# Two feed-forward layers behind a chunk attention: the second layer in a fixed order for each engine, products bank by bank at a block's ends, evictions on one engine

## The chip, the cores and the metric

The kernel runs on one core of a Trainium2 chip. The metric is the device time of one launch in microseconds (us). TensorE (PE) multiplies matrices, VectorE (DVE), ScalarE (ACT) and GpSimd (POOL) work on elements, SyncE (SP) issues the DMA transfers. Each engine works through its own list of instructions in order; semaphores tie the lists together.

## The reference, cut to what matters

```python
# q, k, v: [8 batches, 8 heads, 576, 64]; chunks of 64 positions
scores = scale * np.matmul(q_c, k_c.transpose(0, 1, 2, 4, 3))
attn = np.exp(scores - np.max(scores, axis=-1, keepdims=True))
attn = attn / (np.sum(attn, axis=-1, keepdims=True) + 1e-09)
x = (attn @ v_c), reshaped to [4608 tokens, 512]
h = x @ w_in                                  # layer 1: 512 -> 2048
g = np.maximum(h, 0.0) + alpha * np.minimum(h, 0.0)
x = g @ w_out                                 # 2048 -> 512
h = x @ w_in2                                 # layer 2: 512 -> 2048
g = h - np.tanh(h)
out = g @ w_out2                              # 2048 -> 512
```

All of it is float32. A product of two float32 matrices is made of three products of a high and a low half (high by high, low by high, high by low).

## The kernel before, in words

The 4608 tokens go through in 9 blocks of 512 (NB). The blocks j = 0 to 8 are layer 1, j = 9 to 17 layer 2; layer 1 leaves its results in DRAM (`ysc`) and layer 2 loads them again (`load_y`, L504) and splits them into halves `xh`, `xl` (L508 on ACT, L509 on DVE). The attention of later blocks, the loading and splitting of layer 1's weights and the conversion of layer 2's weights (stored to DRAM as `wm` at L170, fetched and split again from j = 8 on, L153 and L154) are pieces of work that a table of events (`at`, `fire`) places at the steps of the blocks.

A block has 16 steps (KF). Step f makes, for 128 of the 2048 hidden units,

- `up(f)`: 12 matmuls (L420) of 128x512 into one of two PSUM buffers, `hps`;
- `act_g(f)`: the activation, from `hps` to `g` in SBUF. In layer 1 that is two DVE instructions (L441, L444). In layer 2 it is `tanhshrink`: ACT makes `sq` (L460), `th` (L461) and `w` (L462); DVE makes a mask from `sq` (L464; its buffer is `ktc`), then L465, L466, L467, L468 and at last a predicated copy (L469) that picks, element by element, one of two results;
- `split_g`: `g` into two halves, `ghi` on ACT (L450) and `glo` (L451). `glo` is made on DVE in blocks 1 to 8, on POOL in layer 2. In layer 2 the Python code calls `split_g` one step late (`late`);
- `down(f-2)`: 12 matmuls (L478) of the step two before (LAG = 2) into four PSUM banks, `y0` to `y3`, that add up over the block. The first matmuls of a product take `ghi`, its last third `glo`.

The four banks are there once. At a block's end `finish` copies them to SBUF as `yst`, banks 0 and 2 on ACT (L495), banks 1 and 3 on DVE (L497), and SP stores them (L498). Because of the lag, `down(14)` and `down(15)` of a block run in steps 0 and 1 of the next one, and `down(0)` of the next one, in its step 2, is the first that needs the banks empty.

What sets the order: outside a few stretches marked `tc.manual_schedule()` a scheduler arranges the instructions of each engine when the kernel is built. So the order on an engine isn't the order in which Python calls. Inside `tc.manual_schedule()` the order is the program's. Before, only the start of the kernel and its last piece (the last `split_g` and the two last `down`) were marked so. `stage` is a pool of 7 buffers that `sq`, `g` and `yst` share.

Of the kernel before, what the change touches and what calls it, by code (L numbers as in the profile page):

```python
# [27 lines left out]
def kernel(  # L28
# [19 lines left out]
    nc = tc.nc  # L48
# [35 lines left out]
    def slot(f, which, shape, dtype):  # L84
        return wpool.tile(shape, dtype, tag=f"w{which}_{f}", name=f"w{which}_{f}")
# [281 lines left out]
    def att_t_early(t):  # L367

        p = ps.pop(t).rearrange("p h d -> p (h d)")
        tr = ps_h.tile([P, HP, P], F32, tag="h", name="ptr")  # L370
        for hp in range(HP):
            nc.tensor.transpose(tr[:, hp, :], p[:, hp * P:(hp + 1) * P], ident)
        pts[t] = stage.tile([P, HP, P], F32, tag="st", name="pte")
        return nc.scalar.activation(out=pts[t], in_=tr, func=AF.Copy)
# [37 lines left out]
    def up(f, x, n, cols=None, hp=None):  # L412
        if hp is None:
            hp = ps_h.tile([P, n], F32, tag="h", name="hps")
        w = wsplit[f, 0]
        cols = cols or slice(0, n)
        for i, (a, b) in enumerate(((0, 0), (1, 0), (0, 1))):
            for kk in range(KD):
                m = slice(kk * P, (kk + 1) * P)
                nc.tensor.matmul(  # L420
                    out=hp[:, cols], lhsT=w[:, a, m], rhs=x[b][:, kk, cols],
                    start=(kk == 0 and i == 0), stop=(kk == KD - 1 and i == 2),
                )
        return hp

    def act_g(layer, f, hp, n, spare_vector):
        if (layer == 1 or spare_vector) and f % 2:
            g = stage.tile([P, n], F32, tag="st", name="g")
        else:
            g = gpool.tile([P, n], F32, tag="g", name="g", bufs=1)  # L430
        if layer == 1:
            tanhshrink(g, hp, n, f)
        elif spare_vector:
            neg = stage.tile([P, 512], F32, tag="st", name="neg")[:, :n]
            nc.scalar.activation(out=neg, in_=hp, func=AF.Relu, scale=-1.0)
            nc.scalar.activation(out=g, in_=hp, func=AF.Relu)
            nc.vector.scalar_tensor_tensor(
                out=g, in0=neg, scalar=nalpha_sb[:, f:f + 1], in1=g, op0=ALU.mult, op1=ALU.add
            )
        else:  # L440
            nc.vector.tensor_scalar(  # L441
                out=g, in0=hp, scalar1=0.0, scalar2=alpha_sb[:, f:f + 1], op0=ALU.min, op1=ALU.mult
            )
            nc.vector.scalar_tensor_tensor(out=g, in0=hp, scalar=0.0, in1=g, op0=ALU.max, op1=ALU.add)  # L444
        hi = gpool.tile([P, n], F32R, tag="ghi", name="ghi")
        lo = gpool.tile([P, n], F32R, tag="glo", name="glo")
        return g, hi, lo

    def split_g(g, hi, lo, lo_engine):
        nc.scalar.activation(out=hi, in_=g, func=AF.Copy)  # L450
        lo_engine.tensor_tensor(out=lo, in0=g, in1=hi.bitcast(F32), op=ALU.subtract)  # L451

    def tanhshrink(g, hp, n, f):


        ca, cb, ce, cc = TS
        sq = att.tile([P, 2, n], F32, tag="qt", name="sq")[:, 0] if f % 2 else stage.tile([P, n], F32, tag="st", name="sq")
        w = att.tile([P, n], F32, tag=("p", "pt")[f % 2], name="w")
        th = vpool.tile([P, n], F32, tag="v", name="th")
        nc.scalar.activation(out=sq, in_=hp, func=AF.Square)  # L460
        nc.scalar.activation(out=th, in_=hp, func=AF.Tanh)  # L461
        nc.scalar.activation(out=w, in_=sq, func=AF.Square, bias=bias_sb)  # L462
        mask = ktc.bitcast(U32).rearrange("p u h c d -> p (u h c d)")[:, f % 2 * n:(f % 2 + 1) * n]
        nc.vector.tensor_scalar(out=mask, in0=sq, scalar1=0.375 ** 2, scalar2=None, op0=ALU.is_ge)  # L464
        nc.vector.scalar_tensor_tensor(out=g, in0=sq, scalar=cc, in1=hp, op0=ALU.mult, op1=ALU.mult)  # L465
        nc.vector.tensor_tensor(out=th, in0=hp, in1=th, op=ALU.subtract)  # L466
        nc.vector.scalar_tensor_tensor(out=g, in0=w, scalar=ce, in1=g, op0=ALU.add, op1=ALU.mult)  # L467
        nc.vector.scalar_tensor_tensor(out=g, in0=sq, scalar=ca, in1=g, op0=ALU.add, op1=ALU.mult)  # L468
        nc.vector.copy_predicated(g, mask, th)  # L469

    def down(layer, f, g, acc, cuts=((0, 4),)):
        w = wsplit[f, 1]
        for c0, c1 in cuts:
            for i, (u, x) in enumerate(((0, 0), (1, 0), (0, 1))):
                for t in range(c0, c1):
                    m = slice(t * P, (t + 1) * P)
                    lhsT, rhs = (w[:, u, m], g[x + 1]) if layer == 0 else (g[x + 1][:, m], w[:, u])
                    nc.tensor.matmul(  # L478
                        out=acc[t], lhsT=lhsT, rhs=rhs, start=(f == 0 and i == 0), stop=(f == KF - 1 and i == 2)
                    )  # L480
# [5 lines left out]

    ysc = {}

    def finish(layer, j, t0, acc):
        if layer == 0:  # L490
            ysc[j] = dram.tile([KD, P, NB], F32, name=f"ysc{j}")
        for i, a in enumerate(acc):
            st = stage.tile([P, 512], F32, tag="st", name="yst")
            if i % 2 == 0:
                nc.scalar.activation(out=st, in_=a, func=AF.Copy)  # L495
            else:
                nc.vector.tensor_copy(st, a)  # L497
            nc.sync.dma_start(out=ysc[j][i] if layer == 0 else out[t0 + i * P:t0 + (i + 1) * P, :], in_=st)  # L498
# [16 lines left out]
    LAG = 2  # L515
# [32 lines left out]
    for unit in units:  # L548
# [5 lines left out]
        elif t >= 9:  # L554
            last = base[t] - 3
# [26 lines left out]
    for i in range(2 * KF):  # L582
        f, which = divmod(i, 2)
# [17 lines left out]
    def fire(step):  # L601
        for todo in events.pop(step, ()):
            for fn, args in todo:
                fn(*args)

    with tc.manual_schedule():
# [43 lines left out]
        x0 = get_x(0)  # L650
# [46 lines left out]
        last_a = att_t_early(3)  # L697
# [7 lines left out]
        hp0 = up(0, x0, NB, slice(0, 2 * P))  # L705
# [5 lines left out]
        load_natural_early(8, (15, 0))  # L711

    queue, late = [], []

    def next_down():
        layer, f, g, acc, j, t0 = queue.pop(0)
        if f == 0:
            acc.extend(new_acc(layer, NB))
        last = layer == 1 and f == KF - 1
        down(layer, f, g, acc, ((0, 2), (2, 3), (3, 4)) if last else ((0, 4),))  # L720
        if f == KF - 1:
            finish(layer, j, t0, acc)

    for j, (layer, t0) in enumerate(plan):
        x = get_x(j)
        acc = []
        for f in range(KF):
            hp = up(0, x0, NB, slice(2 * P, NB), hp0) if j == f == 0 else up(f, x, NB)
            if len(queue) == LAG:
                next_down()  # L730
            if j == 0:
                if 0 < f < KF - 1:
                    split_w(f + 1, 0, nc.gpsimd)
                if f > 0:
                    split_w(f - 1, 1, nc.gpsimd)
                with tc.issue_after(last_a.ins) if f == 1 else nullcontext():
                    fire(f)
            g = act_g(layer, f, hp, NB, j == 0)
            queue.append((layer, f, g, acc, j, t0))
            if layer == 1:  # L740
                if late:
                    split_g(*late.pop(), nc.gpsimd)
                late.append(g)
            else:
                if j == 1 and f == 0:
                    split_w(KF - 1, 1, nc.gpsimd)
                split_g(*g, nc.gpsimd if j == 0 else nc.vector)
            if j > 0:
                fire(j * KF + f)
    with tc.manual_schedule():  # L750
        split_g(*late.pop(), nc.vector)
        while queue:
            next_down()


# [26 lines left out]
```

## Time and profile before

| | |
|---|---|
| median of 3 runs | 1731.82 us (1729.38 to 1732.12) |
| the profiled execution | 1729.36 us |
| its span, first to last instruction | 1727.6 us |
| PE busy | 1670.8 us, 97%, 9389 matmuls |
| DVE, ACT, POOL busy | 77%, 40%, 20% |
| mean granted TensorE clock | 0.988 of full speed |

Stages by the clock of the span: to about 182 us the start with attention and weights, then layer 1; layer 2 accumulates its first block from 930 us; the last block starts to accumulate at 1637.6 us. A busy share of 97% on PE says that PE is nearly always at work, but a matmul's modelled end overlaps the next one's start, so a small idle time between two matmuls is read from the distance of their starts.

### The profile page before, as it was taken

The page shows a single profiled execution, that of the slowest core. Times are in us where ns is not written, and L with a number is a line of the kernel's source. Part 1 is how long each engine was busy: PE and PEld are TensorE (multiplying, and loading weights), DVE is VectorE, ACT ScalarE, POOL GpSimd, SP SyncE. Part 2 cuts the span into 40 slices and gives each one's busy share as a digit, 9 for nine tenths or more (in the row PEclk, how much of TensorE's full clock was granted, in tenths as well). Part 3 has the DMA queues.
Part 4 walks back from the last instruction along what each step waited for, and adds up shares of the span by engine and source line. Part 5 has one row for each costly group of instructions (what it writes and reads, how often), then busy time and mean ns, then how long its engine had stood idle before and what let it go on. Part 6 is the DMA issues. An engine that isn't in the chain of part 4 may idle for free.

```text
span 1727.6 us, 24773 instructions
## 1 busy us (share of the span) xinstructions
PE 1670.8 (97%) x9389; PEld 1360.8 (79%) x9389; DVE 1324.7 (77%) x2163; ACT 689.5 (40%) x1304; POOL 352.3 (20%) x264
## 2 busy tenths in 40 slices
PE   8877999999999999999999999999999999999998
PEld 7665788788887888888888778888888888888886
DVE  7988866778667868684437797978787878888776
ACT  6665422333322424231334444435353434344433
POOL 3663100000000000000243222222222222222221
PEclk9988999999999999999999999999999999999999
DMA  9811404433153514320422010101010101000000
GB/s 245 253 55 43 133 13 105 116 86 98 50 111 67 156 28 135 57 92 1 146 74 74 1 49 1 49 1 49 1 49 1 49 1 49 1 25 1 25 1 25
DMA packets 215591, 108.58 MB, mean 63 GB/s; under 512 B 170912, under 2 KB 187312, under 8 KB 215472
## 3 DMA queue, kind: packets, MB, share of 16 engines
q1 hardware_dynamic: 215472, 107.01, 22.8%
q8 instruction: 73, 1.20, 0.3%
q14 instruction: 46, 0.38, 0.1%
HBM read 79.70 MB, written 27.26 MB: 62 GB/s over the span
## 4 chain that ended last, share of the span: by engine, by line
PE 51%; DVE 21%; ACT 8%; issue 5%; SPq 3%; DMA 3%; POOL 0%; ACTq 0%; DVEq 0%; POOLq 0%
PE y L478 25%; PE hps L420 24%; DVE g L467 4%; DVE g L469 4%; DVE g L468 4%; DVE g L465 3%; SPq L232 3%; ACT ghi L450 2%; ACT sq L460 2%; DVE ktc L464 2%; ACT w L462 2%; DMA rw<-in_moe_w_in_dram 1%; DVE xl L509 1%; ACT th L461 1%; PE sc L287 1%
## 5 line engine op out<-in xcount | busy, mean ns | idle before, releaser
L420 PE MATMUL hps<-xh,w 128*128 128x512 f32 (+1 forms) x2312 | 589.1, 395 | 18.7 <-DVE g L444 6.2
L420 PEld LDWEIGHTS hps<-xh,w 128*128 128x128 f32 x2312 | 431.1, 189 | 118.2 <-DVE g L444 9.5
L450 ACT ACTIVATE ghi<-g 128x512 fp32r<-128x512 f32 x288 | 181.9, 632 | 721.9 <-DVE g L469 447.6
L451 POOL TENSOR_TENSOR glo<-g,ghi 128x512 fp32r<-128x512 f32 x159 | 218.2, 1372 | 610.4 <-ACT ghi L450 576.7
L420 PE MATMUL hps<-xl,w 128*128 128x512 f32 (+1 forms) x1156 | 311.6, 391 | 0.0
L478 PE MATMUL y<-w,ghi 128*128 128x512 f32 x1152 | 294.2, 393 | 8.2 <-ACT ghi L450 3.7
L478 PE MATMUL y<-ghi,w 128*128 128x512 f32 x1152 | 289.9, 392 | 3.2 <-ACT ghi L450 3.2
L478 PEld LDWEIGHTS y<-w,ghi 128*128 128x128 f32 x1152 | 215.1, 189 | 60.1 <-ACT ghi L450 8.6
L478 PEld LDWEIGHTS y<-ghi,w 128*128 128x128 f32 x1152 | 216.9, 189 | 49.7 <-ACT ghi L450 4.1
L420 PEld LDWEIGHTS hps<-xl,w 128*128 128x128 f32 x1156 | 218.1, 189 | 45.6
L464 DVE TENSOR_SCALAR ktc<-sq 128x512 uint32<-128x512 f32 x144 | 136.3, 947 | 135.0 <-ACT sq L460 135.0
L441 DVE TENSOR_SCALAR g<-hps,alpha_sb 128x512 f32<-128x512 f32 x128 | 95.4, 746 | 93.4 <-PE hps L420 90.8
L332 POOL TENSOR_TENSOR p<-p,rd 128x512 f32<-128x512 f32 x35 | 39.0, 1113 | 618.3 <-DVE rd L331 568.3
L478 PE MATMUL y<-w,glo 128*128 128x512 f32 x576 | 159.1, 389 | 0.0
L478 PE MATMUL y<-glo,w 128*128 128x512 f32 x576 | 157.3, 392 | 0.2 <-POOL glo L451 0.2
L451 DVE TENSOR_TENSOR glo<-g,ghi 128x512 fp32r<-128x512 f32 x129 | 97.3, 754 | 68.8 <-ACT ghi L450 68.5
L478 PEld LDWEIGHTS y<-glo,w 128*128 128x128 f32 x576 | 108.4, 189 | 23.1 <-POOL glo L451 0.6
L478 PEld LDWEIGHTS y<-w,glo 128*128 128x128 f32 x576 | 108.3, 188 | 22.8
L469 DVE COPY_PREDICATED g<-ktc,th 128x512 f32<-128x512 uint32 x144 | 122.9, 853 | 4.4
L467 DVE SCALAR_TENSOR_TENSOR g<-w,g 128x512 f32<-128x512 f32 x144 | 106.6, 741 | 0.0
L462 ACT ACTIVATE w<-sq,bias_sb 128x512 f32<-128x512 f32 x144 | 104.5, 726 | 0.0
L468 DVE SCALAR_TENSOR_TENSOR g<-sq,g 128x512 f32<-128x512 f32 x144 | 100.6, 699 | 4.7
(101 smaller groups left out, 1475.4 us busy)
## 6 DMA issues: line engine op xcount, KB each, us to landing
ysc<-yst SPq DMA_DIRECT2D x36, 256.0 KB, 2.5
yraw<-ysc SPq DMA_DIRECT2D x9, 1024.0 KB, 5.5
out_dram<-yst SPq DMA_DIRECT2D x36, 256.0 KB, 2.5
w<-in_moe_w_in_dram SPq DMA_DIRECT2D x16, 512.0 KB, 6.1
w<-in_moe_w_out_dram SPq DMA_DIRECT2D x16, 512.0 KB, 6.3
rw<-in_moe_w_in_dram SPq DMA_DIRECT2D x32, 256.0 KB, 3.2
rw<-in_moe_w_out_dram SPq DMA_DIRECT2D x32, 256.0 KB, 3.2
w<-wm SPq DMA_DIRECT2D x32, 256.0 KB, 2.1
```

Of the source, the lines that this page charges most:

```text
L232: nc.sync.dma_start(out=o, in_=i)
L420: nc.tensor.matmul(out=hp[:, cols], lhsT=w[:, a, m], rhs=x[b][:, kk, cols], start=(kk == 0 and i == 0), stop=(kk == KD - 1 and i == 2),)
L441: nc.vector.tensor_scalar(out=g, in0=hp, scalar1=0.0, scalar2=alpha_sb[:, f:f + 1], op0=ALU.min, op1=ALU.mult)
L450: nc.scalar.activation(out=hi, in_=g, func=AF.Copy)
L451: lo_engine.tensor_tensor(out=lo, in0=g, in1=hi.bitcast(F32), op=ALU.subtract)
L462: nc.scalar.activation(out=w, in_=sq, func=AF.Square, bias=bias_sb)
L464: nc.vector.tensor_scalar(out=mask, in0=sq, scalar1=0.375 ** 2, scalar2=None, op0=ALU.is_ge)
L465: nc.vector.scalar_tensor_tensor(out=g, in0=sq, scalar=cc, in1=hp, op0=ALU.mult, op1=ALU.mult)
L467: nc.vector.scalar_tensor_tensor(out=g, in0=w, scalar=ce, in1=g, op0=ALU.add, op1=ALU.mult)
L468: nc.vector.scalar_tensor_tensor(out=g, in0=sq, scalar=ca, in1=g, op0=ALU.add, op1=ALU.mult)
L469: nc.vector.copy_predicated(g, mask, th)
L478: nc.tensor.matmul(out=acc[t], lhsT=lhsT, rhs=rhs, start=(f == 0 and i == 0), stop=(f == KF - 1 and i == 2))
```

## The change

Three things change. The steps of a block become two functions, `step_one` for layer 1 and `step_two` for layer 2, and layer 2's blocks run inside `tc.manual_schedule()`. The products `down(0)` and `down(15)` of every block go bank by bank (all three products of bank 0, then of bank 1, and so on); before only the last block's `down(15)` was cut, into banks 0 and 1 together, then 2, then 3. And `finish` is called behind the step's activation and split, with all four evictions on ACT except at the very end, where they alternate as before.

```diff
-    def finish(layer, j, t0, acc):
+    def finish(layer, j, t0, acc, ends=False):
...
-            if i % 2 == 0:
+            if i % 2 == 0 or not ends:
                 nc.scalar.activation(out=st, in_=a, func=AF.Copy)
             else:
                 nc.vector.tensor_copy(st, a)
...
+    SINGLE = ((0, 1), (1, 2), (2, 3), (3, 4))
...
-        last = layer == 1 and f == KF - 1
-        down(layer, f, g, acc, ((0, 2), (2, 3), (3, 4)) if last else ((0, 4),))
+        down(layer, f, g, acc, SINGLE if f in (0, KF - 1) else ((0, 4),))
         if f == KF - 1:
-            finish(layer, j, t0, acc)
+            return lambda ends=False: finish(layer, j, t0, acc, ends)
+        return None
...
+    def step_two(j, t0, f, x, acc):
...
+        hp = up(f, x, NB)
+        done = next_down()
+        g = act_g(1, f, hp, NB, False)
+        queue.append((1, f, g, acc, j, t0))
+        if late:
+            split_g(*late.pop(), nc.gpsimd)
+        late.append(g)
+        if done:
+            done()
+        fire(j * KF + f)
...
+        with tc.manual_schedule() if layer else nullcontext():
+            for f in range(KF):
+                (step_one, step_two)[layer](j, t0, f, x, acc)
     with tc.manual_schedule():
         split_g(*late.pop(), nc.vector)
         while queue:
-            next_down()
+            done = next_down()
+        done(True)
```

ACT in the middle of a block of layer 2, before: the number behind a name is its buffer, and `g_13708` is made by DVE from `sq_13709`, `th_13711` and `w_13710`.

```order
L460 ACTIVATE sq_13709<-hps_13683 128x512
L461 ACTIVATE th_13711<-hps_13683 128x512
L462 ACTIVATE w_13710<-sq_13709,bias_sb_97 128x512
L450 ACTIVATE ghi_13721<-g_13708 128x512
L460 ACTIVATE sq_13751<-hps_13725 128x512
```

Before, the `ghi` of a step stands behind the same step's `w` and ahead of the next step's `sq`.

ACT in layer 2 now, over the two first steps of a block, with the evictions of the block before it:

```order
L460 ACTIVATE sq_13858<-hps_13832 128x512
L461 ACTIVATE th_13860<-hps_13832 128x512
L462 ACTIVATE w_13859<-sq_13858,bias_sb_97 128x512
L450 ACTIVATE ghi_13825<-g_13812 128x512
L460 ACTIVATE sq_13900<-hps_13874 128x512
L461 ACTIVATE th_13902<-hps_13874 128x512
L462 ACTIVATE w_13901<-sq_13900,bias_sb_97 128x512
L450 ACTIVATE ghi_13870<-g_13857 128x512
L495 ACTIVATE yst_13916<-y0_13238 128x512
L495 ACTIVATE yst_13919<-y1_13239 128x512
L495 ACTIVATE yst_13922<-y2_13240 128x512
L495 ACTIVATE yst_13925<-y3_13241 128x512
```

Now the `ghi` behind a step's `w` is that of the step before (`ghi_13870` is of the step that made `sq_13858`), and the four evictions of a block follow in one row.

PE at the same boundary of two blocks, before: `down(15)` of the old block (`w1_15`), `up(2)` of the new one (`w0_2`), and the first product of the new block's `down(0)` (`w1_0`).

```order
L478 MATMUL y2_13220<-w1_15_9134,ghi_13805 128x512 x2
L478 MATMUL y3_13221<-w1_15_9134,ghi_13805 128x512 x2
L420 MATMUL hps_13905<-xh_13421,w0_2_8441 128x512 x4
L478 MATMUL y0_13218<-w1_15_9134,glo_13806 128x512
L478 MATMUL y1_13219<-w1_15_9134,glo_13806 128x512
L478 MATMUL y2_13220<-w1_15_9134,glo_13806 128x512
L478 MATMUL y3_13221<-w1_15_9134,glo_13806 128x512
L420 MATMUL hps_13905<-xh_13421,w0_2_8441 128x512 x4
L420 MATMUL hps_13905<-xl_13422,w0_2_8441 128x512 x4
L478 MATMUL y0_13918<-w1_0_8438,ghi_13847 128x512 x2
```

Before, all four banks are finished by the four `glo` matmuls in the middle of `up(2)`, and eight matmuls of `up(2)` lie between them and `down(0)`. PE there now:

```order
L478 MATMUL y0_13238<-w1_15_9136,ghi_13825 128x512 x2
L478 MATMUL y0_13238<-w1_15_9136,glo_13826 128x512
L478 MATMUL y1_13239<-w1_15_9136,ghi_13825 128x512 x2
L478 MATMUL y1_13239<-w1_15_9136,glo_13826 128x512
L478 MATMUL y2_13240<-w1_15_9136,ghi_13825 128x512 x2
L478 MATMUL y2_13240<-w1_15_9136,glo_13826 128x512
L478 MATMUL y3_13241<-w1_15_9136,ghi_13825 128x512 x2
L478 MATMUL y3_13241<-w1_15_9136,glo_13826 128x512
L420 MATMUL hps_13928<-xh_13441,w0_2_8441 128x512 x8
L420 MATMUL hps_13928<-xl_13442,w0_2_8441 128x512 x4
L478 MATMUL y0_13941<-w1_0_8438,ghi_13870 128x512 x2
```

Now the banks are finished one after the other, three matmuls apart, and the whole of `up(2)` follows. The scheduler had already put `down(0)` bank by bank in layer 2.

SP in block j = 4 of layer 1 (the raw q and k of an attention unit, L232, and the conversion of layer 2's weights, L91, L97 and L170), before:

```order
L170 DMA w_1_7_4999<-wm 128x512
L232 DMA raw<-in_q_dram 32x8x32 x16
L232 DMA raw<-in_k_dram 32x8x32 x16
L97 DMA rw<-in_moe_w_out_dram 128x256
L170 DMA w_0_8_5183<-wm 128x512
```

Now:

```order
L170 DMA w_1_7_4999<-wm 128x512
L97 DMA rw<-in_moe_w_out_dram 128x256 x2
L170 DMA w_0_8_5183<-wm 128x512
L91 DMA rw<-in_moe_w_in_dram 128x2x128 x2
L232 DMA raw<-in_q_dram 32x8x32 x16
L232 DMA raw<-in_k_dram 32x8x32 x16
```

Though layer 1 is still arranged by the scheduler, its order shifts: here the 32 loads of q and k stand behind five more transfers.

## Rows read from the trace of the kernel before

**Rows 1.** The page, busy time of each engine, share of the span, instructions.

```profile
PE 1670.8 (97%) x9389; PEld 1360.8 (79%) x9389; DVE 1324.7 (77%) x2163; ACT 689.5 (40%) x1304; POOL 352.3 (20%) x264
```

**Rows 2.** By stage: length, busy (count) of five engines as above, clock, DMA, GB/s.

```profile
182.00:930.00 748.00, 741.72 (x4800) 606.15 (x4799) 514.58 (x1015) 238.41 (x482) 70.11 (x58) 1.00 0.33 86
1020.90:1637.60 616.70, 612.71 (x2688) 503.11 (x2689) 511.27 (x712) 268.56 (x487) 151.21 (x112) 1.00 0.06 21
```

**Rows 3.** Timeline of PE in layer 2: start, us, engine, line, operation, count.

```profile
1199.92 1.98 PE L420 MATMUL hps<-xh,w 128*128 128x512 f32 x8
...
1227.12 1.98 PE L420 MATMUL hps<-xh,w 128*128 128x512 f32 x8
```

**Rows 4.** Timeline of PE: first `down(0)` matmuls of blocks 9, 10, 17.

```profile
930.01 0.62 PE L478 MATMUL y<-w,ghi 128*128 128x512 f32 x2
...
1020.91 0.73 PE L478 MATMUL y<-w,ghi 128*128 128x512 f32 x2 [0.50 <-ACT yst L495]
...
1637.62 0.71 PE L478 MATMUL y<-w,ghi 128*128 128x512 f32 x2 [1.03 <-DVE yst L497]
```

**Rows 5.** Timeline of ACT, POOL and DVE, one step of layer 2.

```profile
1254.02 0.63 ACT L450 ACTIVATE ghi<-g 128x512 fp32r<-128x512 f32 x1 [3.47 <-DVE g L469]
1254.56 0.58 ACT L460 ACTIVATE sq<-hps 128x512 f32<-128x512 f32 x1
...
1259.70 0.63 ACT L450 ACTIVATE ghi<-g 128x512 fp32r<-128x512 f32 x1 [3.46 <-DVE g L469]
...
1254.73 1.29 POOL L451 TENSOR_TENSOR glo<-g,ghi 128x512 fp32r<-128x512 f32 x1 [4.40 <-ACT ghi L450]
...
1255.17 1.14 DVE L464 TENSOR_SCALAR ktc<-sq 128x512 uint32<-128x512 f32 x1 [1.25 <-ACT sq L460]
...
1258.86 0.74 DVE L469 COPY_PREDICATED g<-ktc,th 128x512 f32<-128x512 uint32 x1
```

**Rows 6.** Timeline of DVE at a catching-up, and of POOL beside it.

```profile
1273.79 0.68 DVE L509 TENSOR_TENSOR xl<-yraw,xh 128x512 fp32r<-128x512 f32 x1
1274.39 0.41 DVE L464 TENSOR_SCALAR ktc<-sq 128x512 uint32<-128x512 f32 x1
...
1278.00 0.41 DVE L464 TENSOR_SCALAR ktc<-sq 128x512 uint32<-128x512 f32 x1
...
1279.53 1.23 DVE L467 SCALAR_TENSOR_TENSOR g<-w,g 128x512 f32<-128x512 f32 x1
...
1278.92 1.29 POOL L451 TENSOR_TENSOR glo<-g,ghi 128x512 fp32r<-128x512 f32 x1 [5.60 <-ACT ghi L450]
```

**Rows 7.** Timeline of ACT and PE at the start of block 15's accumulation.

```profile
1460.56 1.08 ACT L495 ACTIVATE yst<-y 128x512 f32<-128x512 f32 x2
...
1461.20 0.73 PE L478 MATMUL y<-w,ghi 128*128 128x512 f32 x2 [0.49 <-ACT yst L495]
```

**Rows 8.** Timeline of PE and DVE at the end of the program.

```profile
1714.77 3.68 PE L478 MATMUL y<-w,ghi 128*128 128x512 f32 x8 [2.65 <-ACT ghi L450]
...
1720.42 1.19 PE L478 MATMUL y<-w,ghi 128*128 128x512 f32 x4 [1.05 <-ACT ghi L450]
...
1723.05 0.39 PE L478 MATMUL y<-w,glo 128*128 128x512 f32 x1
...
1720.40 0.69 DVE L451 TENSOR_TENSOR glo<-g,ghi 128x512 fp32r<-128x512 f32 x1 [0.76 <-ACT ghi L450]
```

**Rows 9.** The stretch of the last stall but one, columns as in rows 2.

```profile
1714.70:1718.60 3.90, 3.83 (x10) 3.01 (x11) 3.33 (x5) 1.60 (x4) 1.28 (x1) 0.56 0.00 0
```

**Rows 10.** Timeline of PE, SP and DVE in layer 1.

```profile
331.21 2.77 PE L420 MATMUL hps<-xh,w 128*128 128x512 f32 x8 [2.92 <-DVE g L444]
...
526.90 2.11 PE L420 MATMUL hps<-xh,w 128*128 128x512 f32 x8 [1.45 <-DVE g L444]
...
478.81 7.88 SPq L232 DMA_DIRECT2D raw<-in_q_dram  x16
...
517.89 0.71 DVE L272 STREAM_TRANSPOSE ktc<-raw 128x512 f32<-128x512 f32 x1 [5.38 <-DMA raw<-in_k_dram]
```

More of the change, by code (lines that the diff above doesn't have):

```diff
@@ L718, in next_down, with step_one @@
             acc.extend(new_acc(layer, NB))
-        last = layer == 1 and f == KF - 1
-        down(layer, f, g, acc, ((0, 2), (2, 3), (3, 4)) if last else ((0, 4),))
+        down(layer, f, g, acc, SINGLE if f in (0, KF - 1) else ((0, 4),))
         if f == KF - 1:
-            finish(layer, j, t0, acc)
+            return lambda ends=False: finish(layer, j, t0, acc, ends)
+        return None
+    def step_one(j, t0, f, x, acc):
+        hp = up(0, x0, NB, slice(2 * P, NB), hp0) if j == f == 0 else up(f, x, NB)
+        done = next_down() if len(queue) == LAG else None
+        if j == 0:
+            if 0 < f < KF - 1:
+                split_w(f + 1, 0, nc.gpsimd)
+            if f > 0:
+                split_w(f - 1, 1, nc.gpsimd)
+            with tc.issue_after(last_a.ins) if f == 1 else nullcontext():
+                fire(f)
+        g = act_g(0, f, hp, NB, j == 0)
+        queue.append((0, f, g, acc, j, t0))
+        if j == 1 and f == 0:
+            split_w(KF - 1, 1, nc.gpsimd)
+        split_g(*g, nc.gpsimd if j == 0 else nc.vector)
+        if done:
+            done()
+        if j > 0:
+            fire(j * KF + f)
[7 more added lines that the diff above has]
+        late.append(g)
+        if done:
+            done()
+        fire(j * KF + f)
     for j, (layer, t0) in enumerate(plan):
@@ L726 @@
         acc = []
-        for f in range(KF):
-            hp = up(0, x0, NB, slice(2 * P, NB), hp0) if j == f == 0 else up(f, x, NB)
-            if len(queue) == LAG:
-                next_down()
[L731 to L749, printed above, removed]
+        with tc.manual_schedule() if layer else nullcontext():
+            for f in range(KF):
+                (step_one, step_two)[layer](j, t0, f, x, acc)
     with tc.manual_schedule():
@@ L752 @@
         while queue:
-            next_down()
+            done = next_down()
+        done(True)
 _INS = ["q", "k", "v", "moe_w_in", "moe_w_out", "moe_alpha", "moe2_w_in", "moe2_w_out"]
```

## The prediction

> **What bounds the kernel now.** I read the page's busy times first: PE is busy for 97% of the span, DVE for 77%, ACT and POOL for far less [rows 1]. So the time can fall only where PE stands still or is slowed, and the question is where it does and whether the change touches those places. The table by stage answers the first half roughly: the granted clock is 1.00 both from 182 to 930 us, where PE is busy 741.72 of 748.00 us, and from 1020.90 to 1637.60 us, with 612.71 of 616.70 us [rows 2]. Busy time flatters PE, because a matmul's modelled end overlaps the next start; so I read the distance of starts. In the timeline of PE, 120 matmuls of layer 2 run undisturbed from 1199.92 to 1227.12 us [rows 3]: 27.20 / 120 = 0.2267 us each, 5.44 us for a step of 24, 87.04 us for a block of 384.
>
> Against that floor the starts of `down(0)` [rows 4] show what layer 2 loses. First block: 1020.91 - 930.01 = 90.90, less 87.04, is 3.86 us. The next seven: 1637.62 - 1020.91 = 616.71, less 2688 x 0.22667 = 609.28, is 7.43 us. Last block up to the last matmul at 1723.05 us [rows 8]: 85.43, less 347 x 0.22667 = 78.65, is 6.78 us. Together 18.07 us. This is all that the change can win in layer 2.
>
> Why is it lost? The timelines of ACT and DVE show a loop through two engines [rows 5]. ACT's `ghi` begins at 1254.02 us and the next step's `ghi` at 1259.70 us, 5.68 us later, which is 0.24 us more than PE's 5.44. Between them ACT sits idle for 3.46 us, released by DVE's L469. ACT's next `sq` starts only behind that `ghi`, DVE's mask L464 behind that `sq` (1.25 us idle), and the chain of DVE runs to L469, for which the next `ghi` waits. So DVE and ACT lose 0.24 us a step to PE; once per block the scheduler had let `sq` pass, and DVE catches up: there L464 follows L464 after 3.61 us [rows 6]. While the backlog lasts, evictions and `ghi` come late at the block's end.
>
> **The change part by part.** *The fixed order on ACT* puts `sq`, `th`, `w` of step f ahead of `ghi` of f-1. Call T the end of `up(f)`. `sq` needs 0.5 us, so DVE starts the mask near T + 0.65. Its six instructions undisturbed take 3.61 us from mask to mask [rows 6], so `g` is ready near T + 4.3. The next `sq` is not behind this `ghi` any more: the loop is cut. What is late next? `ghi(f)` comes behind `w(f+1)`, that is one step later and three ACT instructions in, up to T + 5.44 + 2.24 = T + 7.7; POOL's `glo(f)` takes 1.29 us [rows 5] and ends near T + 9.0. `down(f)` stands behind `up(f+2)` and starts at T + 2 x 5.44 = T + 10.9: 3 us of slack for the one, 2 us for the other. The PSUM buffer `hps` is read last by L466 at about T + 2.4 and needed again at T + 8.1. So PE should run at 5.44 us a step.
>
> The cover for this is DVE's own rate. It must stay under 5.44 us: 3.61 plus 0.60 for the `xl` of four of the sixteen steps (1273.79 to 1274.39 us [rows 6]) is 3.76 on average. What can be added is blocking by POOL. L464 takes 0.41 us alone, and 1.14 us when it begins 0.44 us behind a POOL instruction; it ends 0.29 us after that one [rows 5, 6]. L467 was stretched to 1.23 us beside `glo` and ended 0.55 us after it [rows 6]. One `glo` a step can thus cost DVE at most its own 1.29 us: 3.76 + 1.29 = 5.05 us, under 5.44. Measured before, all blocking included, DVE is busy for 511.27 / 112 steps = 4.56 us [rows 2]. I cost the shift at nothing; with xl and full blocking in one step it is 5.50 us, 0.06 late, given back in the next.
>
> The Trainium skill has a rule here (SBUF — State Buffer, section "Who interferes with whom"): a DVE instruction that reads two inputs from SBUF, or runs in a two-port mode, shares a pair of ports with GpSimd, and the one that comes second is blocked for the whole instruction, while one with at most one SBUF input goes free. The trace agrees: L464 1.14 against 0.41 us. The rule speaks against the change, as `glo` now begins near L466 and L467, which reads two tiles of SBUF, instead of beside the short mask. By it the sum would still be 5.05 us on DVE; without it, 3.76.
>
> *Evictions on ACT and bank by bank.* At the start of block 15 PE waits 0.49 us for L495 [rows 7], with eviction pairs 1.08 us long begun at 1460.56; it loses 0.66 to 0.77 at each of these seven starts (of the 7.43). Now bank 0 is complete three matmuls into `down(15)` and bank 3 at its end; the whole `up(2)`, 2.72 us, lies behind it, and `down(0)` needs the banks 0.68 us apart. Four evictions of 0.54 us (1.08 for two) follow `ghi` on ACT: from T + 2.24 to T + 4.4 of the block's step 1, where `down(0)` starts at T + 5.44 and needs the last bank only at T + 7.5. Loss: nothing; bounds 0 and, as now, 7 x 0.77 = 5.4. ACT has room: 268.56 / 112 = 2.40 us a step [rows 2], and two more evictions of 0.54 in 16 steps add 0.07 us a step.
>
> *First block of layer 2.* ACT also splits the last weights there, and the four `yst` need free buffers of a shared pool. Should that put `ghi` some 3 us late for a step or two, the slack above takes up nearly all. I take 0.3 us; the bounds are 0 and today's 3.86.
>
> *The end.* PE now waits 2.65 us for `ghi(14)` [rows 8], and the stretch behind has a granted clock of 0.56, the lower of its two levels [rows 9], so eight matmuls take 3.68 instead of the 1.98 us of rows 3. Then 1.05 us for `ghi(15)`. In the new order `ghi(14)` is done near T + 2.24 of step 15, before `down(14)` starts at T + 2.72, and `glo(14)` near T + 3.6, before its first matmul at T + 4.5. `down(15)` would start at T + 5.44; `g(15)` is ready at T + 4.3, or 5.5 with `glo(14)` blocking DVE, `ghi(15)` 0.6 us and `glo(15)`, 0.69 us on DVE [rows 8], follow. Bank by bank the first `glo` matmul is the third, 0.45 us in. That is 0 to 0.9 + 0.4 us; I take 1.2. A wait of 1.05 us left the rate of matmuls as it was (four in 1.19 us [rows 8]), so I book nothing for the clock. From the last matmul to the end of the span stay the same 4.5 us, since the last eviction is DVE's, as before.
>
> *Layer 1* isn't in the fixed order, but its order shifts. In block 4 the 32 loads of q and k are issued behind five more transfers on SP's queue; they began at 478.81 us, and DVE's transpose waited 5.38 us for the last of them, until 517.89 us [rows 10]; eight us more there is the price of a repeat of that wait if no slack lies ahead. Two stalls there could also vanish: 2.92 us at 331.21 and 1.45 us at 526.90 [rows 10]. Against PE's rate I see some 8 us of such stalls. Value taken: 0; bounds -8 and +6.
>
> **Sum.** 18.07 - 0.3 - 1.2 = 16.6 us. Span 1727.6 - 16.6 = 1711.0; with the 1.8 us outside it, 1712.8 us against the profiled execution's 1729.36. The median shown, 1731.82, lies 2.5 us above that execution, so the same kernel reads 1712.8 to 1715.3: I predict 1714 us.
>
> **Rivals.**
> (a) *The block ends still cost.* Four evictions in a row on one engine stand behind `ghi(0)`; if DVE is late, so is `ghi`, and the banks with it. For: PE waits for L495 at each start today. Against: 2.72 us of `up(2)` now lie between. Price 5.4 us: 1719 to 1720 us.
> (b) *Layer 1 takes the gain back.* SP's queue is in order, and the loads of block 4 are later. For: the wait of 5.38 us says that they were late already. Against: PE passed that wait with 1.45 us at most. Price 6 to 16 us: 1720 to 1730, no change at the upper end.
> (c) *Slower: DVE becomes the bound.* If POOL holds DVE up for long in every step (at L467, and through a late L468 again in the next), DVE's 3.76 us grows beyond 5.44; it decides from 1.68 us of blocking a step. With the 5.68 us of today's loop and no catching-up, 144 x 0.24 = 34.6 less the 18.07 already paid is +16.5: 1727.6 + 16.5 + 1.8, or 1747 us by the median. For: `glo` moves to the instructions that it can block. Against: 1.29 us is all that POOL holds, and 4.56 us is what DVE took.
> (d) *The change isn't what it says:* the scheduler's order was as good, the 0.24 us is PE's own. Then 1731 us. Rows 3 speak against it.
>
> **How the numbers follow.** Chances: forecast 0.74, (a) 0.10, (b) 0.09, (c) 0.05, (d) 0.02. About 0.2%, 3.5 us, is what a measurement of this kernel can tell from no change. Forecast, (a) and half of (b) are faster: 0.88; the rest of (b) and (d) give 0.06 for the same, (c) and a tail of (b) 0.06 for slower. The forecast with layer 1's -8 gives 1706, and (a) and the middle of (b) reach 1722: the range is 1706 to 1722.
>
> **What would show it.** Right: `down(0)` starts 87.0 to 87.2 us apart from the second block of layer 2 on; no idle time of PE released by `yst`; DVE's mask every 5.44 us and 0.41 us long; the clock at 1.00 through the last 15 us. Wrong: steps above 5.44 us with DVE never idle (c); PE released by L495 (a); a stall near 525 us several us long (b).

## The result, and the profile after

The kernel after takes 1712.34 us (median of 4 runs, 1710.61 to 1713.03) against 1731.22 before (4 runs): a ratio of 0.9892, 95% interval 0.988 to 0.9905. The forecast was 1714 us, range 1706 to 1722. The profiled execution took 1710.61 us, its span is 1708.8 us, 18.8 less than before.

The page's busy times, as in [rows 1]:

```profile
PE 1663.6 (97%) x9389; PEld 1364.1 (80%) x9389; DVE 1369.4 (80%) x2129; ACT 705.2 (41%) x1338; POOL 351.3 (21%) x264
```

DVE is busy for 45 us more than before, with the same instructions but for the evictions moved to ACT, and the kernel is faster. Busy time of an engine off the path tells nothing by itself.

By stretch, layer 1 and the seven middle blocks of layer 2 (columns as in [rows 2]):

```profile
182.00:927.30 745.30, 741.16 (x4803) 605.83 (x4802) 506.15 (x995) 242.73 (x492) 64.92 (x54) 1.00 0.32 84
1015.10:1624.40 609.30, 609.30 (x2689) 504.50 (x2688) 555.52 (x701) 276.47 (x504) 148.67 (x112) 1.00 0.07 25
```

The second row is the result in one line: 609.30 us for seven blocks, PE busy in all of it. Before, the same work took 616.71.

The timeline of PE, the first `down(0)` matmuls of blocks 9, 10 and 17, and the end, which answer to [rows 4, 8]:

```profile
927.35 0.62 PE L478 MATMUL y<-w,ghi 128*128 128x512 f32 x2
...
1015.13 0.62 PE L478 MATMUL y<-w,ghi 128*128 128x512 f32 x2
...
1624.41 0.62 PE L478 MATMUL y<-w,ghi 128*128 128x512 f32 x2
...
1699.66 1.07 PE L478 MATMUL y<-w,glo 128*128 128x512 f32 x4
1701.73 0.73 PE L478 MATMUL y<-w,ghi 128*128 128x512 f32 x2 [1.00 <-ACT ghi L450]
...
1704.65 0.40 PE L478 MATMUL y<-w,glo 128*128 128x512 f32 x1
```

The differences of these starts split the 18.8 us. Up to the first product of layer 2: 930.01 to 927.35, 2.7 us won. First block: 90.90 to 87.78, 3.1. Seven blocks: 616.71 to 609.28, 7.4. Last block up to its last matmul: 85.43 to 80.24, 5.2. From there to the end: 4.53 to 4.18, 0.4.

One step in the middle of layer 2, ACT, POOL and DVE, which answers to [rows 5, 6]:

```profile
1303.65 0.60 ACT L460 ACTIVATE sq<-hps 128x512 f32<-128x512 f32 x1 [2.71 <-PE hps L420]
1305.23 0.63 ACT L450 ACTIVATE ghi<-g 128x512 fp32r<-128x512 f32 x1
1309.09 0.60 ACT L460 ACTIVATE sq<-hps 128x512 f32<-128x512 f32 x1 [3.22 <-PE hps L420]
...
1305.94 1.30 POOL L451 TENSOR_TENSOR glo<-g,ghi 128x512 fp32r<-128x512 f32 x1 [4.14 <-ACT ghi L450]
...
1304.34 0.42 DVE L464 TENSOR_SCALAR ktc<-sq 128x512 uint32<-128x512 f32 x1
1305.98 1.80 DVE L467 SCALAR_TENSOR_TENSOR g<-w,g 128x512 f32<-128x512 f32 x1
1308.55 0.75 DVE L469 COPY_PREDICATED g<-ktc,th 128x512 f32<-128x512 uint32 x1
1309.72 0.43 DVE L464 TENSOR_SCALAR ktc<-sq 128x512 uint32<-128x512 f32 x1 [0.43 <-ACT sq L460]
```

Read who releases whom. Before, ACT's `ghi` was released by DVE and `sq` stood behind it; now `ghi` waits for nothing, and `sq`, 5.44 us apart, waits for PE's `up`. The loop between DVE and ACT is gone. POOL's `glo` now begins 0.04 us ahead of L467 and stretches it to 1.80 us; the mask L464 is back at 0.42.

ACT and PE at the start of block 16's accumulation, as in [rows 7]:

```profile
1534.24 2.06 ACT L495 ACTIVATE yst<-y 128x512 f32<-128x512 f32 x4
...
1537.37 0.62 PE L478 MATMUL y<-w,ghi 128*128 128x512 f32 x2
```

All four evictions are over 1.07 us before `down(0)` begins, and PE's row has no wait.

### The profile page after: what moved, and what is told of

It reads as the page before. It is cut to its first block, busy times and chain, and to the rows that moved or that the text cites. A ratio compares the mean times of both kernels' runs of the same rounds, so it can differ in the third digit from the quotient of the medians.

```text
span 1708.8 us, 24770 instructions
## 1 busy us (share of the span) xinstructions
PE 1663.6 (97%) x9389; PEld 1364.1 (80%) x9389; DVE 1369.4 (80%) x2129; ACT 705.2 (41%) x1338; POOL 351.3 (21%) x264
## 4 chain that ended last, share of the span: by engine, by line
PE 75%; SPq 5%; DVE 3%; DMA 3%; issue 3%; ACT 1%; POOL 1%; DVEq 0%; ACTq 0%; POOLq 0%
PE hps L420 37%; PE y L478 37%; SPq L232 4%; DMA rw<-in_moe_w_out_dram 1%; DMA rw<-in_moe_w_in_dram 1%; PE sc L287 1%; DMA raw<-in_k_dram 1%; PE sc L358 1%; ACT wm L107 0%; DMA ysc<-yst 0%; DVE ktc L272 0%; DVE g L441 0%; DVE qt L272 0%; POOL w L154 0%; DVE g L444 0%
## 5 line engine op out<-in xcount | busy, mean ns | idle before, releaser
L478 PE MATMUL y<-ghi,w 128*128 128x512 f32 x1152 | 296.0, 391 | 3.5 <-ACT ghi L450 3.0
L460 ACT ACTIVATE sq<-hps 128x512 f32<-128x512 f32 x144 | 86.2, 598 | 416.6 <-PE hps L420 415.8
L467 DVE SCALAR_TENSOR_TENSOR g<-w,g 128x512 f32<-128x512 f32 x144 | 243.1, 1688 | 0.0
L478 PE MATMUL y<-glo,w 128*128 128x512 f32 x576 | 164.7, 392 | 0.3 <-POOL glo L451 0.3
L478 PE MATMUL y<-w,glo 128*128 128x512 f32 x576 | 162.8, 389 | 0.0
L468 DVE SCALAR_TENSOR_TENSOR g<-sq,g 128x512 f32<-128x512 f32 x144 | 111.3, 773 | 5.0
L469 DVE COPY_PREDICATED g<-ktc,th 128x512 f32<-128x512 uint32 x144 | 108.9, 756 | 4.9
L465 DVE SCALAR_TENSOR_TENSOR g<-sq,hps 128x512 f32<-128x512 f32 x144 | 99.0, 688 | 11.9
```

The costliest lines, as they stand in the source:

```text
L478: nc.tensor.matmul(out=acc[t], lhsT=lhsT, rhs=rhs, start=(f == 0 and i == 0), stop=(f == KF - 1 and i == 2))
```

## The experiments

Each ratio is to the kernel before on the same chip. Three chips were used, on which the kernel before has medians of 1728.67, 1730.01 and 1732.35 us, so a difference between medians of runs on different chips is good to some 3 us; where less than that matters, the starts in the traces decide. The kernel after was measured a second time on the chip of the last three runs.

**The order given back.** Layer 2 goes to the scheduler again; cuts and evictions stay.

```diff
-        with tc.manual_schedule() if layer else nullcontext():
+        with nullcontext():
```

> The kernel after, with layer 2's blocks handed back to the scheduler; the cuts bank by bank and the evictions on ACT stay. Theory A (the gain of layer 2 is the fixed order, which cuts the loop between DVE and ACT of 5.68 us a step): the loop comes back, PE loses 0.24 us a step with one catching-up a block, and the 2.65 us wait for ghi at the end; at most the waits at the seven block starts (7 x 0.77 = 5.4 us) stay gone. 18.1 - 2.3 lost again, less 0 to 5.4: 1722 to 1728 us against 1712. Theory B (the gain came from the blocks' ends, that is from cuts and evictions): it stays within 3 us of the kernel after, 1710 to 1716.

Measured: 1747.1 us (1745.32 to 1748.44), ratio to before 1.0103 (1.0089 to 1.0117). That is 35 us above the kernel after, and slower than the kernel before, which neither theory had. The mask's and `ghi`'s rows show the loop again, about 5.7 us from `ghi` to `ghi`, as in [rows 5]. In the timeline of PE there are two more waits in each block:

```profile
1283.28 2.11 PE L420 MATMUL hps<-xh,w 128*128 128x512 f32 x8 [1.28 <-DVE th L466]
...
1290.81 1.07 PE L420 MATMUL hps<-xl,w 128*128 128x512 f32 x4
1293.13 1.21 PE L420 MATMUL hps<-xh,w 128*128 128x512 f32 x4 [1.25 <-DVE th L466]
```

Two `up` now follow each other, and PE waits for an `hps` buffer that DVE has not read yet. A block takes 91.0 us, 16 x 5.68, where it took 88.1 before. So the gain needs the fixed order: without it the other two parts are a loss. Why the scheduler arranges `up` like this around the moved `finish` was not tried further.

**The loop put back, nothing else.** The program's order, but with a step's own `ghi` behind its `w`.

```diff
-        if late:
-            split_g(*late.pop(), nc.gpsimd)
-        late.append(g)
+        if j == 2 * n1 - 1 and f == KF - 1:
+            late.append(g)
+        else:
+            split_g(*g, nc.gpsimd)
```

> The kernel after, with ghi and glo of a step made in the same step of layer 2 (ACT in the order sq, th, w, ghi of one step), still in the program's order, so that nothing can pass and catch up. Theory A: ACT's next sq stands behind the ghi for which DVE's last instruction is awaited; every step takes the loop's 5.68 us instead of PE's 5.44: 143 x 0.24 = 34 us more than the kernel after, 1744 to 1750 us, L464 back at 1.14 us and waiting for sq. Theory B (no loop; the step of 5.68 was the scheduler's doing at the blocks' ends): within 5 us of 1712.

Measured: 1775.68 us (1772.18 to 1778.39), ratio 1.0268 (1.0254 to 1.0282): 63 us above the kernel after instead of 34. The direction holds, and the loop is there, but the size was too small. ACT and PE at a block's start:

```profile
1308.62 0.63 ACT L450 ACTIVATE ghi<-g 128x512 fp32r<-128x512 f32 x1 [3.45 <-DVE g L469]
1309.16 2.04 ACT L495 ACTIVATE yst<-y 128x512 f32<-128x512 f32 x4
1311.07 0.62 ACT L460 ACTIVATE sq<-hps 128x512 f32<-128x512 f32 x1
...
1309.79 0.73 PE L478 MATMUL y<-w,ghi 128*128 128x512 f32 x2 [2.19 <-ACT yst L495]
```

Once ACT is in the loop, everything in its list is: the four evictions, 1.9 us up to the next `sq`, lengthen it, and PE waits for them. The two blocks from 1122.23 to 1309.79 us take 93.8 us each, 2.9 more than 16 x 5.68 = 90.9, and the evictions make 1.9 of that. ACT's rows inside such a block show two more terms:

```profile
1275.71 0.58 ACT L460 ACTIVATE sq<-hps 128x512 f32<-128x512 f32 x1
1281.39 0.62 ACT L508 ACTIVATE xh<-yraw 128x512 fp32r<-128x512 f32 x1
1281.91 0.58 ACT L460 ACTIVATE sq<-hps 128x512 f32<-128x512 f32 x1
...
1293.40 0.58 ACT L460 ACTIVATE sq<-hps 128x512 f32<-128x512 f32 x1
1294.96 0.60 ACT L460 ACTIVATE sq<-hps 128x512 f32<-128x512 f32 x1
...
1303.50 0.58 ACT L460 ACTIVATE sq<-hps 128x512 f32<-128x512 f32 x1
```

Four steps of a block also have an `xh` ahead of the next `sq` and take 6.2 us from `sq` to `sq`, some 0.5 more. And where one block's fixed stretch ends and the next one's begins, an `sq` passes a `ghi`: the two steps there take 10.1 us, 1.3 less than twice 5.68. So the expectation's "nothing can pass" holds inside a block alone, and of all these terms it had counted only the 0.24 us a step. Of the 63 us the seven middle blocks make 45.5 (654.81 us against 609.28).

**Layer 2 without cuts; then with alternating evictions.**

```diff
-        down(layer, f, g, acc, SINGLE if f in (0, KF - 1) else ((0, 4),))
+        down(layer, f, g, acc, (SINGLE if layer == 0 else ((0, 2), (2, 3), (3, 4)) if j == 2 * n1 - 1 and f else ((0, 4),)) if f in (0, KF - 1) else ((0, 4),))
```

> The kernel after, with down(0) and down(15) of layer 2's blocks in one cut of four banks (layer 1 and the last down(15) keep theirs, the latter as before the change). Theory A: the banks are all complete within the last 0.9 us of down(15), ACT evicts them from about 2.6 to 4.8 us behind its start, and down(0) needs them at 5.44: the cuts in layer 2 buy nothing, 1710.5 to 1714 us. Theory B: the seven starts lose 0.5 to 0.77 us each again, 1716 to 1718.

Measured: 1710.61 us (1708.98 to 1714.29), ratio 0.9896 (0.9882 to 0.9909). The cuts buy nothing in layer 2 while ACT evicts. The other half:

```diff
-            if i % 2 == 0 or not ends:
+            if i % 2 == 0 or layer == 0:
```

> The kernel after, with layer 2's evictions alternating between ACT and DVE as before (layer 1 all on ACT). Theory A: DVE's two copies stand behind L469 of the block's second step, done near 6.0 and 6.7 us behind the start of down(15), while banks 1 and 3 are needed at 6.1 and 7.5: a loss of 0 to 0.3 us a block and 1.4 us more DVE work in that step, which its slack of 0.8 us a step takes up by the third step: 1711 to 1715 us. Theory B: the evictions on ACT carried the gain at the blocks' ends, 1716 to 1718.

Measured: 1714.67 us (1712.6 to 1716.18), ratio 0.9915 (0.9902 to 0.9929). By the trace PE waits once per block, for DVE's copy of bank 1:

```profile
1279.57 1.27 DVE L497 COPY yst<-y 128x512 f32<-128x512 f32 x2
...
1280.30 0.73 PE L478 MATMUL y<-w,ghi 128*128 128x512 f32 x2 [0.19 <-DVE yst L497]
```

The middle blocks are 87.52 us apart here, 0.48 more than the floor: 4 us over the layer, between the 0.3 and the 0.77 that the theories had. The intervals of the two ratios overlap, so the times alone don't tell it from the kernel after; the starts do.

**The fixed order alone**, on the kernel before: old cuts, alternating evictions, layer 1 untouched. In layer 2 `finish` keeps its new place, behind a step's activation and split. Beside that, of layer 2's part of the change this leaves only

```diff
+        with tc.manual_schedule() if layer else nullcontext():
+            for f in range(KF):
+                (step_one, step_two)[layer](j, t0, f, x, acc)
```

> The kernel before with the fixed order of layer 2 alone: cuts and engines of the evictions as before in both layers, layer 1 instruction for instruction as before. Theory A (the fixed order alone breaks the loop): the first start of down(0) about 2.6 us later than in the kernel after, as before; DVE's copies of banks 1 and 3 stand behind the L469 of a block's second step, done near 6.0 and 6.7 us after down(15) began, and uncut down(0) needs them by 5.7 and 6.1: 0.5 us lost a block, 8 x 0.5 = 4, and the last 1.2. Near 1717 us (1714 to 1720). Theory C (the parts need each other, as the scheduler with the two other parts alone was 18 us slower than before): the order without the cuts gives less than half of the gain, 1721 us or more.

Measured: 1726.3 us (9 runs, 1721.87 to 1727.55), ratio 0.9975 (0.9966 to 0.9985): a fifth of the gain. Theory A's 1717 failed; theory C's 1721 or more, less than half of the gain, is what came. DVE and PE at a block's start:

```profile
1283.30 0.74 DVE L469 COPY_PREDICATED g<-ktc,th 128x512 f32<-128x512 uint32 x1
1283.94 1.27 DVE L497 COPY yst<-y 128x512 f32<-128x512 f32 x2
...
1283.63 0.39 PE L478 MATMUL y<-w,ghi 128*128 128x512 f32 x1
1284.67 2.02 PE L478 MATMUL y<-w,ghi 128*128 128x512 f32 x7 [0.65 <-DVE yst L497]
```

In a fixed order DVE's two copies stand behind L469, and uncut `down(0)` asks for bank 1 after its first matmul on bank 0. PE loses 1.08 us at each start (the blocks are 88.12 us apart), and 3.33 us at the start of the first block, where the copies of block 8's banks are awaited. Within blocks the steps run at 5.44. So the order removes the loop, but the seven middle blocks win nothing by it: 616.77 us, against 616.71 before. Of the 18.07 us at stake in layer 2 the order alone wins 4.9, most of it in the last block (81.01 us instead of 85.43). What the evictions cost at a start depends on the other two parts: 1.08 us as here, 0.48 with cuts, nothing on ACT, with or without cuts. That DVE's copies stand behind L469 comes from the new place of `finish`; the old place in a fixed order was not run.

**Evictions on ACT alone**, on the kernel before, layer 2 only.

```diff
-            if i % 2 == 0:
+            if i % 2 == 0 or layer == 1 and j < 2 * n1 - 1:
```

> The kernel before with layer 2's evictions on ACT alone (all but the last block's); the scheduler still orders layer 2 and cuts are as before. Theory A: evictions matter only through the order that the scheduler makes around them. With four copies on ACT, sq goes ahead of ghi in other places than before; where no sq passes a ghi, a block takes 16 x 5.68 = 91 us as in the run with the scheduler and both other parts, against 88.1 before: up to 8 x 2.8 = 22 us slower, 1730 to 1752 us. Theory B (evictions on ACT free the block's start by themselves): 7 x 0.77 = 5 us faster, 1722 to 1725.

Measured: 1728.32 us (11 runs, 1725.76 to 1730.23), ratio 0.9994 (0.9986 to 1.0003): no change. Neither theory's number: the blocks stay 88.1 us apart and PE waits 0.45 to 0.50 us for L495 at the seven starts from 1020 to 1549 us, as in [rows 7]. With the loop in place ACT is late whoever evicts.

**Layer 1 exactly as before, layer 2 as after** (cuts, evictions and the place of `finish`):

```diff
-        down(layer, f, g, acc, SINGLE if f in (0, KF - 1) else ((0, 4),))
+        down(layer, f, g, acc, SINGLE if layer == 1 and f in (0, KF - 1) else ((0, 4),))
...
-            if i % 2 == 0 or not ends:
+            if i % 2 == 0 or layer == 1 and not ends:
...
+        if done:
+            done()
...
-        if done:
-            done()
```

> The kernel after in layer 2 (fixed order, cuts, evictions on ACT), with layer 1 instruction for instruction as before. The two profiles put the start of layer 2's first product at 930.0 us before and 927.4 after. Theory A (the shifted order of layer 1 gave 2 to 3 us): 2 to 3 us above the kernel after, 1714 to 1716. Theory D (that difference is what two executions of one kernel differ by): 1710 to 1713.

Measured: 1715.47 us (1715.34 to 1715.58), ratio 0.9921 (0.9908 to 0.9935): 3 us above the kernel after by the medians, 5 by the ratios (0.9892 there). One of these is plain in the trace: block 8's evictions on DVE, in the first block of layer 2.

```profile
934.73 0.73 PE L478 MATMUL y<-w,ghi 128*128 128x512 f32 x2 [1.20 <-DVE yst L497]
```

That block takes 89.04 us, 1.3 more than in the kernel after. The rest lies in layer 1, see below.

**Layer 1 in the program's order too.**

```diff
-        with tc.manual_schedule() if layer else nullcontext():
+        with tc.manual_schedule():
```

> The kernel after with layer 1 in the program's order as well. Theory A: a fixed order pays where it takes a wait out of a loop, as in layer 2; in layer 1 the program's order puts weight conversions and attention pieces of a step behind its activation, DVE is busy 69% and POOL little, and nobody has arranged them for it: each step in which PE then waits for L444 costs 0.5 to 3 us; I expect 5 to 40 us slower than after, 1717 to 1752. Theory E (a fixed order is better as such, the scheduler was the loss): the 7 us of stalls in layer 1 vanish, 1705 to 1709.

Measured: 1759.44 us (1759.12 to 1761.39), ratio 1.018 (1.0166 to 1.0194): 47 us above the kernel after, somewhat more than I had expected. By the starts 28 us of it are lost before the second block of layer 1 (its first `up` begins at 196.9 us instead of 168.6). PE's long waits are for attention's pieces; in its timeline the largest two beyond 200 us are

```profile
513.48 0.90 PE L251 MATMUL tr<-ident,rawn 128*128 128x128 f32 x3 [5.49 <-DVE qt L253]
...
733.77 0.48 PE L251 MATMUL tr<-ident,rawn 128*128 128x128 f32 x1 [5.72 <-DVE qt L253]
```

A fixed order is no gain as such.

**POOL's blocking removed, and doubled.** First `glo` on DVE:

```diff
-            split_g(*late.pop(), nc.gpsimd)
+            split_g(*late.pop(), nc.vector)
```

> The kernel after with layer 2's glo made on DVE instead of POOL, behind the step's L469. In the kernel after, L467 takes 1.71 us on average against 0.68 beside nothing, as POOL's glo begins just ahead of it. Theory A (that blocking lies in DVE's slack): DVE needs 3.76 + 0.65 = 4.4 us a step instead of 4.8, L467 is back at 0.68 us, and the time stays that of the kernel after, 1709 to 1714 us, as PE alone paces it. Theory F (the blocking costs PE a little in every step): 144 x 0.03 to 0.05 us less, 1704 to 1708.

Measured: 1716.32 us (1713.01 to 1718.33), ratio 0.9905 (0.9891 to 0.992). L467 is back at 0.68 us, and the middle blocks are 87.04 us apart as in the kernel after: the blocking cost PE nothing there. The time isn't lower but, if anything, higher (the second measurement of the kernel after, on the same chip, has 1712.27), for DVE is late in the first block of layer 2, which takes 90.43 us instead of 87.78:

```profile
938.20 0.98 PE L478 MATMUL y<-w,glo 128*128 128x512 f32 x3 [2.96 <-DVE glo L451]
```

Then each `glo` twice on POOL:

```diff
-            split_g(*late.pop(), nc.gpsimd)
+            split_g(*late[0], nc.gpsimd)
+            g2, hi2, lo2 = late.pop()
+            nc.gpsimd.tensor_tensor(out=lo2, in0=g2, in1=hi2.bitcast(F32), op=ALU.subtract)
```

> The kernel after with POOL making each glo of layer 2 twice over (the same values a second time), which doubles what can block DVE. Theory A (DVE's own time must pass 5.44 us a step before PE feels it, and one glo blocks it for 1.03): 3.76 + 2 x 1.03 = 5.8 us a step, 0.4 above PE's: 144 x 0.2 to 0.4 us more than the kernel after, 1735 to 1770. Theory G (a second POOL instruction finds a DVE instruction that doesn't need the port, or the 0.4 us that DVE idles): under 5 us more, 1711 to 1716.

Measured: 1717.76 us (1716.03 to 1719.05), ratio 0.9915 (0.9902 to 0.9927). Theory A's 1735 or more failed; theory G is nearer. By groups from 1005 to 1614 us, the kernel after (`a2`, the second measurement) and then this one (count, busy us, mean ns, idle before):

```profile
L467 DVE SCALAR_TENSOR_TENSOR g<-w,g 128x512 f32<-128x512 f32 x112 | 191.1, 1706 | 0.0
L468 DVE SCALAR_TENSOR_TENSOR g<-sq,g 128x512 f32<-128x512 f32 x112 | 84.3, 753 | 3.9
L464 DVE TENSOR_SCALAR ktc<-sq 128x512 uint32<-128x512 f32 x112 | 47.7, 426 | 36.6 <-ACT sq L460 36.6
```

```profile
L468 DVE SCALAR_TENSOR_TENSOR g<-sq,g 128x512 f32<-128x512 f32 x113 | 187.6, 1660 | 3.9
L467 DVE SCALAR_TENSOR_TENSOR g<-w,g 128x512 f32<-128x512 f32 x112 | 154.9, 1383 | 0.0
L464 DVE TENSOR_SCALAR ktc<-sq 128x512 uint32<-128x512 f32 x112 | 46.5, 415 | 0.0
```

The two instructions together are blocked for 0.70 + 0.97 = 1.67 us a step, and L464 never waits: DVE is full, 579.52 of 587.00 us from 1020 to 1607. Yet PE is busy in all 587.00 of them. The trace shows why, at a step with an `xl` (L509) and the one ahead of it:

```profile
1220.13 1.53 DVE L467 SCALAR_TENSOR_TENSOR g<-w,g 128x512 f32<-128x512 f32 x1
1224.04 0.68 DVE L509 TENSOR_TENSOR xl<-yraw,xh 128x512 fp32r<-128x512 f32 x1
1226.17 0.94 DVE L467 SCALAR_TENSOR_TENSOR g<-w,g 128x512 f32<-128x512 f32 x1
...
1219.82 1.30 POOL L451 TENSOR_TENSOR glo<-g,ghi 128x512 fp32r<-128x512 f32 x1 [2.46 <-ACT ghi L450]
1225.26 1.30 POOL L451 TENSOR_TENSOR glo<-g,ghi 128x512 fp32r<-128x512 f32 x1 [2.45 <-ACT ghi L450]
```

POOL starts behind ACT's `ghi`, here 5.44 us apart although DVE is late. Before the `xl` its `glo` begins 0.31 us ahead of L467, which takes 1.53 us; the `xl` makes DVE 0.6 us later, the next `glo` begins 0.91 us ahead of L467 and runs for the greater part beside L465 and L466, which it doesn't stretch (0.68 us in both kernels), and L467 takes 0.94. The step with the `xl` takes DVE 6.02 us from mask to mask, the next one 4.85, and it has caught up (masks at 1218.61, 1224.63 and 1229.48 us). So when DVE falls behind, the blocking shrinks to what it can bear. The cost lies in the first steps of layer 2, where PE waits four times for `glo`, 2.5 us in all, and once at the end, 0.8 us.

**No cuts in either layer.**

```diff
-        down(layer, f, g, acc, SINGLE if f in (0, KF - 1) else ((0, 4),))
+        down(layer, f, g, acc, ((0, 2), (2, 3), (3, 4)) if layer == 1 and j == 2 * n1 - 1 and f == KF - 1 else ((0, 4),))
```

> The kernel after without the cuts bank by bank in either layer (the last block's as before the change); the fixed order and the evictions on ACT stay. Theory A (cuts and evictions on ACT do the same work, one of them is enough): as the run without cuts in layer 2, 1710 to 1714; layer 1's order shifts once more, which is worth -2 to +4. Theory B (layer 1 needs its cuts): 9 block starts of layer 1 lose 0.3 to 0.7 us each, 1714 to 1718.

Measured: 1711.71 us (1710.71 to 1713.99), ratio 0.9878 (0.9863 to 0.9894), level with the kernel after on the same chip:

> The kernel after once more, unchanged, on the chip of the three other runs of this call, as their measure: 1710 to 1714 us. Its layer 1, by the starts of up in the first block of layer 2, 913.8 us in the first profile: theory D (executions of one program differ by a clock that falls in some of them behind the stall near 330 us) 913 to 916.5; otherwise within 0.5 of 913.8.

Measured: 1712.27 us (1711.67 to 1713.23), ratio 0.9884 (0.987 to 0.9898). The cuts are worth nothing that can be measured as long as ACT evicts; no version here beats the kernel after.

## Why the prediction was right

**The loop.** It was the right reading of layer 2: in the kernel after a step takes 5.44 us, seven blocks 609.28 us, and putting the loop back alone costs 63 us, more than was at stake, since in that run the evictions and `xh` lengthen it. The 18.1 us at stake became 0.74 in the first block (0.3 forecast) and 1.59 in the last (1.2 forecast), none between; 15.7 us won where 16.6 were forecast.

**The evictions and cuts.** "Loss: nothing" holds, but the text gave both edits the credit. The runs without cuts show that the evictions on ACT do it alone once the order is fixed; the cuts halve the loss (1.08 to 0.48 us a block) only where DVE evicts. Nor is the gain a sum of the parts: in the seven middle blocks the order alone and the evictions alone win nothing, both together all of the 7.4 us. Rival (a) did not come: PE waits for no eviction. With the order alone 8 x 1.08 = 8.6 us stay at the block starts, more than its 5.4, but by DVE's two copies and not by four in a row on ACT.

**The end.** The 2.65 us wait for `ghi(14)` is gone, and with it the stretch at the lower clock [rows 9]: the granted clock is 1.00 from 1694 to the last matmul. The wait for `ghi(15)` is 1.00 us, a little above the 0 to 0.9 of the forecast; by the starts it costs 1.16, and the waits for `glo(15)` behind it 0.43, near the 0.4 that was sized. From the last matmul to the end the span won 0.4 us where the same 4.5 were forecast. That is the cut's: the two runs that differ from the kernel after in cuts alone have 4.5 us there. The cut takes 0.3 of it back ahead of the last matmul (80.24 us for the last block, 79.98 and 79.95 in those two).

**The blocking.** "At most its own 1.29 us" fits: L467 takes 1.71 us on average, 1.03 more than alone, and DVE is busy for 4.96 us a step (555.52 / 112), under 5.44. The rule of the Trainium skill (SBUF — State Buffer, "Who interferes with whom") told rightly which instruction would suffer, one with two SBUF inputs and not L465 or L466. L464, on which the forecast saw the rule at work, reads one tile of SBUF, so its 1.14 us fit the rule only if the mask runs in a two-port mode; its 0.41 us alone, against 0.68 of the instructions with two inputs, speaks for that, but no run shows it. Rival (c)'s turning point, 1.68 us of blocking a step, was all but reached in the run with `glo` twice, at 1.67, without a loss in the steady steps, and the rows there show the blocking shrink by itself when DVE is late.

**Layer 1.** The forecast was 0; the profile shows 2.7 us won. The starts of block 9's first `up` tell how far to trust that: 916.4, 916.2, 915.3 and 917.2 us in the four profiles where layer 1 is as before, 913.8, 914.8, 916.0, 914.9, 914.2, 915.3, 914.1 and 917.0 us in the eight where it is as after. The means differ by 1.3 us, the ranges overlap. Part of the spread is one stall of PE near 330 us, behind which the matmuls went at about half the rate in some profiles and not in others. In the kernel after:

```profile
330.15 1.20 PE L420 MATMUL hps<-xh,w 128*128 128x512 f32 x4 [2.73 <-DVE g L444]
...
329.00:335.00 6.00, 4.85 (x21) 4.04 (x22) 4.92 (x12) 2.56 (x6) 1.32 (x1) 1.00 0.41 66
```

After 2.73 us of idle time the clock stays at 1.00; before, after 2.92 us, eight matmuls took 2.77 us instead of 1.98 [rows 3, 10]. Behind this stall the clock fell in all four profiles with layer 1 as before, and in four of the eight with it as after. Those four (916.0, 915.3, 914.1 and 917.0 us) have a mean of 915.6 against 916.3: like beside like, 0.7 us is left for the order of layer 1, which the overlapping ranges don't tell from nothing. Whether the order has a part in when the clock falls stays open. Rival (b) did not come: PE has no wait of several us near 525.

**The sum.** Execution against execution the forecast was 1712.8 us, and the profiled one took 1710.61. The 2.2 us are layer 1's 2.7, less 0.9 that layer 2 gave short, and 0.4 behind the last matmul. Part of the 2.7 is luck of this pair of executions: the clock fell behind the stall near 330 us in the one before and not in the one after. The median lies 1.7 us above that execution; 2.5 had been allowed, as before.

## What to carry to other kernels

Where an engine's list holds a wait for a second engine ahead of work that the second engine needs, the two form a loop; its length is read from start to start in the timeline of either, and it counts as soon as it is longer than the bound engine's step, here by 0.24 us of 5.68. Break it by issuing the awaited work one step late, and then look at what else stands in the same lists, for the evictions took back all that the middle blocks had to give until they went to the engine that had become free. A part that does nothing alone (the evictions), or costs alone (the scheduler with the other parts), may still be needed beside another, so undo parts from the whole as well as adding them to the start.

## What the runs showed of the hardware

POOL's `glo` and a DVE instruction with two SBUF inputs exclude each other in both directions: L467 takes 0.68 us alone and 1.80 us when POOL began 0.04 us ahead, and POOL's second `glo` takes 1.62 us on average instead of 1.29 when L467 is under way. That doubling POOL's work filled DVE to 99% without slowing PE was not expected. The clock behind the stall near 330 us can't be told from the stall's length: in the two profiles of the kernel after PE idled 2.73 and 2.72 us and the matmuls behind it started every 227 ns, the granted clock at 1.00; in the run with layer 1 as before it idled 2.65 us, in the run with the order alone 2.23 us, and behind it matmuls started every 427 ns, the granted clock at 0.50, the lower of its two levels.
